# A linear-attention and MLP kernel: the first layer of units 3 to 11 in seven products of 64-row tiles, with its inputs laid out by heads

## The chip, the cores and the metric

The kernel runs on one core of one Trainium2 chip. The metric is the device time of one execution in microseconds (us), the median of several runs. A core has TensorE (PE, matrix products from SBUF into PSUM), VectorE (DVE), ScalarE (ACT), GpSimd (POOL) and SyncE (SP, which here only issues DMAs). Every engine works through its own instructions in order and waits on semaphores for the others.

## What is computed

```python
def _attn_ref(r, k, v, w, u):                    # all (4, 8, 768, 48) float32, u (8, 48)
    for t in range(S):
        cur = np.einsum('bhd,bhe->bhde', u[None] * kt, vt)
        y[:, :, t] = np.einsum('bhd,bhde->bhe', rt, state + cur)
        state = wt[:, :, :, None] * state + np.einsum('bhd,bhe->bhde', kt, vt)
x = y.transpose(0, 2, 1, 3).reshape(3072, 384)
h = x @ w_in                                     # (384, 2048)
out = (h * (1.0 / (1.0 + np.exp(-h)))) @ w_out   # (2048, 384), float32
```

An attention with a decaying state (4 batches, 8 heads of 48, 768 tokens) gives x; two matrix products with a silu between them follow. All is float32.

## The kernel before

**Tiling.** A unit is 128 tokens of two batches, 256 rows of x; six stretches of tokens and two pairs of batches make 12 units, 0 to 11. Attention is not run token by token: decays are multiplied up over 128 tokens, scores (128 x 128 for each head) come from PE, the state enters once a unit. x is kept transposed, features on partitions, 384 = 3 chunks (KC) of 128, 256 columns (two halves of 128, one for each batch).

**Order.** The order is written out by hand and each engine keeps it. Iteration i of the main loop (i from 3) emits in turns the groups of attention steps of unit i (`mix`), and the steps of the second layer of unit i-2 (`downs`: seven `quarter` products) and of the first layer of unit i-1 (`ups`); the tuple `room` says how many matrix steps follow each group. Iterations 0 to 2 are written singly; they also convert the weights (loaded in eight pieces for each matrix, `load_weight`) with `head_weight`, `tail_weight`, `join_weight` and, on GpSimd, `add_weight` (L259).

**Attention steps that matter here.** `turn` transposes r, k and w; `product`, `grow_*`, `prepare` multiply decays (L616 on DVE, L634 and L643 on GpSimd, L604 on ACT); `burst` and `keep_level` make scores (L692, L700 on PE; L710 on DVE; the score copies, L792, on ACT). The bonus u is a chain of its own: `block_bonus` (L491, eight products on GpSimd: four for the next unit ahead of `y_state`, four in this one), `block_sum` (L525, DVE), `block_move` (three DMAs), `block_spread` (L552, four ACT copies and a shuffle on DVE), `block_write` (L561, two predicated DVE copies into the scores). Then `turn_apart` and `turn_k` (kq, the keys for the state, ACT copies from PSUM), `y_state` (L835) and `y_values` (L856) on PE, four ACT copies of y to `yt` (L861), and `update` of the state (L896). `yt` has heads on rows 0 to 47 and 64 to 111; `move_x` (L914) makes x of it with ten DMAs from SBUF to SBUF, for units from 4 on issued by ACT.

**Matrix steps.** Units 0 to 2 run the first layer plainly (`up`, L1011; 24 products of 128 x 128 weights and 256 columns, silu at L1020). From unit 3 on (NFAST) `first_layer` (L1065) splits two of the three chunks with the two batches and the two halves of the 2048 columns after Strassen and Winograd, seven products for eight; the third chunk is folded in plainly. So each half of 1024 columns takes 11 products of 8 tiles, each tile 128 rows x 64 columns of weights by 128 moving columns, two tiles side by side on the two column halves of PE. `sums_of_x` (L1039, DVE, five 128 x 128 subtractions) makes d1 to d4 of x, `in_weight_sums` makes s1, s2, s4 and a21 of w_in once, in iterations 3 and 4. Each product ends in two halves' evacuation: an ACT copy (p1, p6, p5, L1074), a DVE add into gt and an ACT silu (n1, p7, p3, L1077, L1080), or a silu alone (p4, L1082). Four PSUM banks are kept for this: h0, h1 (p_h) and o0, o1 (p_o). The second layer's `sums` (L1127, DVE) and `quarter` (L1156 on PE, evacuations L1161 and below) follow one iteration later.

**Loads.** All loads and stores are issued by SP. Values (`load_values`) have two buffers and are loaded a unit ahead; the blocks of r, k and w are spread over the groups of an iteration.

```python
    for i in range(3, len(units)):
        steps = downs(i - 2) + ups(i - 1)
        groups = mix(i)
        if i - 1 >= NFAST:
            groups[3].append((sums_of_x, i - 1))
...
        for group, count in zip(groups, room):
            do(*group)
            for step in steps[:count]:
                do(*step)
            steps = steps[count:]
```

Of the kernel before, what the change touches and what calls it, by code (L numbers as in the profile page):

```python
# [8 lines left out]
F32 = mybir.dt.float32  # L9
# [29 lines left out]
def kernel(  # L39
# [11 lines left out]
    nc = tc.nc  # L51
# [44 lines left out]
    WRK = {"w": 0, "r": 1, "k": 2}  # L96
    vt, vq, whole = {}, {}, {}
# [32 lines left out]
    def load_values(i):  # L130
# [3 lines left out]
        rooms = [pin.tile([128, H * D + PD - D], F32, name=name, bufs=2) for name in ("vt", "vq")]  # L134
        if n == 0:
            for room in rooms:
                nc.vector.memset(room[:, H * D:], 0.0)
        whole[i] = rooms
        vt[i], vq[i] = (room[:, 0:H * D].rearrange("p (h d) -> p h d", h=H) for room in rooms)
# [66 lines left out]
    def load_weight(i):  # L206
        dst, src = w_ends[i]
        if rounded:
            dst, src = staged(i).rearrange("p (c f) -> p c f", c=src.shape[1]), src.bitcast(U32)
        nc.sync.dma_start(out=dst, in_=src)  # L210
# [603 lines left out]
    def turn_k(i):  # L814
        both_kq = pt.tile([128, NB, NP, 2 * PD], F32, name="kq", bufs=1)
        for b in range(NB):
            kq[i, b] = both_kq[:, b]
        for e, have in enumerate(apart[i]):
            nc.scalar.copy(out=both_kq[:, :, :, PD * e:PD * e + D], in_=have)
# [30 lines left out]
    def y_values(i, e):  # L850
# [7 lines left out]
        if e == 0:  # L858
            yt[i] = pt.tile([128, NP, NB, L], F32, name="yt", bufs=1)
        for x in range(2):  # L860
            nc.scalar.copy(out=yt[i][PD * e:PD * e + D, x::2, :, :],  # L861
                           in_=p_yt[i, e][PD * x:PD * x + D].rearrange("p (q b) t -> p q b t", b=NB))
# [3 lines left out]
    def x_products(i, b):  # L866

        if b == 0:
            xt[i] = pt.tile([128, KC, TU], F32, name="xt", bufs=1)
        to = p_x[i, b] = ps.tile([128, KC, L], F32, name="p_h", bufs=2) if i == 0 else bank("p_m", KC, L)  # L870
        have = whole[i][b]
        places = []
        for c in range(KC):
            for row in range(0, 128, PD):
                at = c * 128 + row
                last = (at + PD - 1) // D
                assert at // D == last - 1
                places += [(c, row, last, PD), (c, row, last - 1, last * D - at)]
        places.sort(key=lambda place: -place[3])
        for c, row, h, columns in places:  # L880
            at = c * 128 + row
            nc.tensor.matmul(to[row:row + columns, c, :], lhsT=have[:, at:at + columns],
                             rhs=score[:, i % NSC, h % 2, b * NP + h // 2, :], start=True, stop=True)
# [4 lines left out]
    def update(i, b):  # L888
# [5 lines left out]
        for p in range(NP):  # L894
            for e in range(2):
                nc.tensor.matmul(p_kv[i][PD * e:PD * e + D, b, p, :], lhsT=kq[i, b][:, p, PD * e:PD * e + D],  # L896
# [17 lines left out]
    def move_x(i, first=0, last=None, queue=nc.sync):  # L914

        if i not in xt:
            xt[i] = pt.tile([128, KC, TU], F32, name="xt", bufs=1)
        moves = []
        for h in range(H):
            at = h * D  # L920
            while at < (h + 1) * D:
                end = min((h + 1) * D, (at // 128 + 1) * 128)
                row = PD * (h % 2) + at - h * D
                moves.append((xt[i][at % 128:at % 128 + end - at, at // 128, :],
                              yt[i][row:row + end - at, h // 2].rearrange("p b t -> p (b t)")))
                at = end
        for to, have in moves[first:last]:
            queue.dma_start(out=to, in_=have)
# [9 lines left out]
    def mix(i):  # L938
# [15 lines left out]
        def start(j):  # L954
# [3 lines left out]
               [*at(i < len(units) - NB, (turn_apart, i), (turn_k, i)), (y_state, i), *both(y_values, i), *at(ahead, *turns(i + 1)),  # L958
                (sums, i - 1, FH // 2 - 2 if i - 1 < NFAST else 0), *both(update, i), *at(not ahead, (move_x, i))]]
# [11 lines left out]
        else:  # L971
            groups = [[*both(turn, i, "r"), (grow_own, i, 0), (move_x, i - 1, 0, 2, nc.scalar)],
                      [*start(i), *sum_steps(i, 0, 1), *bonus_steps(i, 4, 5), (move_x, i - 1, 2, None, nc.scalar)],
# [10 lines left out]
        if i + 1 < len(units):  # L984
            loads.insert(len(loads) // 2, (load_values, i + 1))
# [36 lines left out]
    HALF = DF // 2  # L1022
    whole_w = raw[:, 1].rearrange("p x b h d -> p x (b h d)")
    in_sums = [whole_w[:, WRK["r"]], const.tile([128, HALF], F32, name="in_sum"), whole_w[:, WRK["w"]]]
    a11, a12, a13 = (w_in_sb[:, c, 0:HALF] for c in range(KC))
    a21, a22, a23 = (w_in_sb[:, c, HALF:DF] for c in range(KC))
    x_sums = [spare[:, at + x * L:at + (x + 1) * L] for x in range(3)] + [const.tile([128, L], F32, name="x_sum")]

    def in_weight_sums(which):
        out, one, two, op = ((in_sums[0], a21, a22, ALU.add), (in_sums[1], in_sums[0], a11, ALU.subtract),  # L1030
                             (in_sums[2], a12, in_sums[1], ALU.subtract), (a21, a11, a21, ALU.subtract))[which]
# [284 lines left out]
```

## Time and profile before

| | |
|---|---|
| device time of three runs | 588.21, 590.79, 591.96 us; median 590.79 |
| span of the profiled execution, first to last instruction | 588.6 us (the page gives no other time for it) |
| granted TensorE clock | 1.000 throughout |
| busy in the span | PE 97%, DVE 77%, POOL 60%, ACT 45% |
| 0 to 100 us (units 0, 1, weights converted) | PE 93.98 busy |
| 100 to 189.37 us (to the start of unit 3's first layer) | PE 88.34 of 89.37 busy |
| seven stretches from one unit's first layer to the next, 189.37 to 505.33 | 45.58, 44.34, 45.82, 45.58, 45.31, 44.52, 44.81 us |
| the last such stretch, 505.33 to 547.44 | 42.11 us, all of it PE busy |
| tail, 547.44 to 588.60 | PE 37.83 busy |

The stretches are read from the chain of waits, in which every unit's p1 starts with the same row, and their busy times from a table of windows. An engine's idle time is put down to what released it ("<-PE p_sc L692"). "PEld" is the loading of weights, which runs beside the products. A float32 product is recorded as two passes, so the profile counts 8070 where the program has 4132 products (a few records are missing).

### The profile page before, as it was taken

What the parts mean: (1) busy time and instruction counts of PE and PEld (TensorE: products, weight loads), DVE (VectorE), ACT (ScalarE), POOL (GpSimd) and SP (SyncE); (2) the same over time, 40 slices, a digit from 0 to 9 for tenths busy, and PEclk for the clock granted to TensorE, in tenths of its full rate; (3) what the DMA queues carried; (4) which work ended last, traced back from release to release, by engine and by line L of the source; (5) the groups of instructions that cost most, each with busy time, mean ns of one, the idle gap of its engine ahead of it and who ended that gap; (6) DMA issues with size and microseconds to landing.
All of it is one profiled execution on the core that took longest, in us unless ns stands there. A gap on an engine that the chain in (4) does not pass through costs nothing.

```text
span 588.6 us, 19384 instructions
## 1 busy us (share of the span) xinstructions
PE 573.7 (97%) x8070; PEld 533.3 (91%) x8070; DVE 455.7 (77%) x703; ACT 264.2 (45%) x582; POOL 354.1 (60%) x415
## 2 busy tenths in 40 slices
PE   8989999999999999999999999999999989999997
PEld 8767876798899989999999989999999989999997
DVE  7979789998898898787788898888678797861150
ACT  5679694431531561561561561460470462370320
POOL 5989778357768478287486496485676677500000
PEclk9999999999999999999999999999999999999999
DMA  9957785343432643544543544444354460100000
GB/s 231 311 122 195 167 244 82 47 86 70 102 68 39 133 71 53 131 66 75 114 68 60 123 62 68 105 75 73 85 100 71 95 102 27 38 7 24 28 3 26
DMA packets 203383, 53.70 MB, mean 91 GB/s; under 512 B 186784, under 2 KB 195104, under 8 KB 203296
## 3 DMA queue, kind: packets, MB, share of 16 engines
q1 hardware_dynamic: 197360, 48.73, 41.0%
q10 hardware_dynamic: 5936, 3.74, 2.4%
q8 instruction: 63, 1.03, 0.8%
q14 instruction: 24, 0.20, 0.1%
HBM read 43.21 MB, written 5.24 MB: 82 GB/s over the span
## 4 chain that ended last, share of the span: by engine, by line
PE 76%; SPq 5%; DVE 5%; POOL 4%; DMA 4%; ACT 3%; issue 1%; ACTq 1%; POOLq 0%; DVEq 0%
PE p_o L1156 26%; PE p_h L1065 16%; PE p_o L1065 8%; PE p_h L1011 8%; PE p_h L1156 4%; PE p_m L1095 4%; PE p_m L856 2%; PE p_sc L692 2%; DVE score L561 2%; SPq L127 2%; PE p_m L835 2%; DMA vq<-in_v_dram 2%; ACT score L792 2%; POOL w_in_sb L259 2%; POOL tk L634 1%
## 5 line engine op out<-in xcount | busy, mean ns | idle before, releaser
L634 POOL TENSOR_TENSOR tk<-tk,tw 128x256 f32<-128x256 f32 x128 | 91.3, 734 | 42.8 <-ACT tk L604 27.6
L491 POOL TENSOR_TENSOR ruk<-tokens_rk 128x768 f32<-128x768 f32 (+1 forms) x32 | 53.6, 1687 | 70.9 <-DVE block_sums L525 36.6
L1156 PE MATMUL p_o<-own,temps 128*128 128x192 f32 x528 | 88.8, 327 | 1.3 <-ACT partial L1161 1.3
L1156 PEld LDWEIGHTS p_o<-own,temps 128*128 128x128 f32 x528 | 86.0, 190 | 2.5 <-ACT partial L1161 2.4
L1011 PE MATMUL p_h<-xt,w_in_sb 128*128 128x256 f32 x288 | 66.1, 384 | 1.7 <-POOL w_in_sb L259 1.5
L1065 PE MATMUL p_h<-xt,w_in_sb 128*64 128x128 f32 x1008 | 62.8, 274 | 0.4 <-issue 0.4
L1011 PEld LDWEIGHTS p_h<-xt,w_in_sb 128*128 128x128 f32 x288 | 53.6, 190 | 10.0 <-POOL w_in_sb L259 2.4
L1156 PE MATMUL p_o<-w_out_sb,gt 128*128 128x192 f32 x340 | 59.9, 329 | 0.2 <-DVE temps L1127 0.2
L616 DVE TENSOR_TENSOR tr<-tr,tw 128x512 f32<-128x512 f32 x61 | 57.3, 939 | 2.6 <-PE p_m L692 2.1
L1065 PEld LDWEIGHTS p_h<-xt,w_in_sb 128*64 128x64 f32 x1008 | 55.8, 137 | 2.0 <-issue 0.9
L1156 PEld LDWEIGHTS p_o<-w_out_sb,gt 128*128 128x128 f32 x340 | 55.3, 190 | 2.0 <-issue 1.2
L1161 ACT COPY partial<-p_o 128x192 f32<-128x192 f32 x33 | 10.6, 320 | 95.7 <-PE p_o L1156 46.5
L406 POOL TENSOR_TENSOR tw<-tw 128x256 f32<-128x256 f32 (+6 forms) x83 | 40.0, 482 | 17.7 <-DVE tw L360 13.8
L1065 PE MATMUL p_o<-xt,w_in_sb 128*64 128x128 f32 x720 | 46.9, 273 | 0.0
L604 ACT COPY tk<-tk 128x256 f32<-128x256 f32 x52 | 21.2, 407 | 53.8 <-POOL tk L634 49.2
L1065 PEld LDWEIGHTS p_o<-xt,w_in_sb 128*64 128x64 f32 x720 | 40.8, 137 | 0.0
L1074 ACT COPY gt<-p_h 128x512 f32<-128x512 f32 x45 | 26.2, 582 | 30.4 <-PE p_h L1065 30.4
L1080 ACT ACTIVATE gt<-gt 128x512 f32<-128x512 f32 x36 | 22.7, 631 | 34.1 <-DVE gt L1077 33.9
L710 DVE COPY_PREDICATED score<-mask,p_sc 128x512 f32<-128x512 int8 x42 | 31.3, 800 | 5.8 <-PE p_sc L692 5.5
L1077 DVE TENSOR_TENSOR gt<-p_o,gt 128x512 f32<-128x512 f32 x27 | 18.4, 683 | 19.4 <-PE p_o L1065 19.4
L1077 DVE TENSOR_TENSOR gt<-p_h,gt 128x512 f32<-128x512 f32 x27 | 18.6, 687 | 17.3 <-PE p_h L1065 16.2
L643 POOL TENSOR_TENSOR tk<-tk,tw 128x256 f32<-128x256 f32 x32 | 30.9, 986 | 0.0
(225 smaller groups left out, 1272.0 us busy)
## 6 DMA issues: line engine op xcount, KB each, us to landing
w_out_sb<-in_moe_w_in_dram SPq DMA_DIRECT2D x6, 768.0 KB, 7.1
w_out_sb<-in_moe_w_out_dram SPq DMA_DIRECT2D x4, 768.0 KB, 5.1
own<-in_moe_w_out_dram SPq DMA_DIRECT2D x4, 768.0 KB, 5.8
tokens_rk<-in_r_dram SPq DMA_DIRECT2D x8, 384.0 KB, 4.4
tokens_rk<-in_k_dram SPq DMA_DIRECT2D x8, 384.0 KB, 5.3
tokens_w<-in_w_dram SPq DMA_DIRECT2D x8, 384.0 KB, 6.4
raw<-in_w_dram SPq DMA_DIRECT2D x80, 32.0 KB, 2.3
raw<-in_k_dram SPq DMA_DIRECT2D x80, 32.0 KB, 2.1
```

The lines of the kernel that those rows point to most:

```text
L406: engine.tensor_tensor(out=up, in0=t[:, :, 0::2], in1=t[:, :, 1::2], op=ALU.mult)
L491: mul = lambda out, one, two: nc.gpsimd.tensor_tensor(out=out, in0=one, in1=two, op=ALU.mult)
L616: nc.vector.tensor_tensor(out=odd, in0=odd, in1=tw[i][l][:, :, 0::2][:, :, :, None].to_broadcast([128, Q, L >> (l + 1), c]), op=ALU.mult)
L634: nc.gpsimd.tensor_tensor(out=out, in0=have, in1=odd_products(i, l, b, *blocks), op=ALU.mult)
L643: nc.gpsimd.tensor_tensor(out=have, in0=have, in1=odd_products(i, l, b, [2, NP * ni]), op=ALU.mult)
L710: nc.vector.copy_predicated(out=dst, mask=masks[l][:, :, None].to_broadcast([128, NB, NP, ni, c]), data=sc[e].rearrange("p (b q) (i c) -> ...
L1011: nc.tensor.matmul(p_h[:, a, :], lhsT=w_in_sb[:, c, f * 128:(f + 1) * 128], rhs=xt[i][:, c, :], start=(c == 0), stop=(c == KC - 1))
L1065: nc.tensor.matmul(p[h:h + PD, q, :], lhsT=left[:, f:f + PD], rhs=right, start=first and n == 0 and q == 0, stop=last and n == len(pairs) ...
L1074: nc.scalar.copy(out=g(*{"p1": (0, 0), "p6": (0, 1), "p5": (1, 1)}[name]), in_=p)
L1077: nc.vector.tensor_tensor(out=to, in0=p, in1=to, op=ALU.add)
L1095: nc.tensor.matmul(po[i, b], lhsT=gt[i, f // 2][:, f % 2, b * L:(b + 1) * L], rhs=w_out_sb[:, f, :], start=(f == 0), stop=(f == FC - 1))
L1156: nc.tensor.matmul(p, lhsT=left(f), rhs=right[:, f, :], start=which in (0, 1, 3) and f == 0, stop=f == FH - 1, skip_group_check=True)
```

## The change

From unit 3 on all three chunks are split. x and the rows of w_in are laid out by heads: chunk c has head 2c on rows 0 to 47 and head 2c+1 on rows 64 to 111, and 16-row slices of heads 6 and 7 on rows 48 to 63 and 112 to 127. `load_weight` reads w_in in four DMAs for a piece in place of one, in that order of rows. The 64-row halves of this layout are the inner split of the products: `first_layer` has seven products (p1, p2, p6, p5, p7, p3, p4), each of 3 chunks x 4 blocks of 128 columns x 2 halves of the outer columns, in tiles of 64 rows x 128 columns; the two halves alternate between the two row halves of PE and go to two PSUM banks. For that, the two 64-row halves of some blocks of w_in change places once (`swap_out` in iteration 3, `swap_in` in iteration 4: DMAs within SBUF), and each half of x is copied to the other row half as well (`spread_x`, two ACT copies a unit). `in_weight_sums` is now two DVE operations of 128 x 1536 and, on GpSimd, one of 128 x 1536 and three of 128 x 512, all in iteration 4. `sums_of_x` is four subtractions of 128 x 384 and stands in group 4, behind the block sums and `block_move`, where it stood in group 3.

y goes from PSUM straight into x (`x_rooms`) for six of eight heads, by ACT (`y_out`, six copies); only heads 6 and 7 pass through `yt`, and `move_x` is six DMAs of 16 rows on SP. For units 0 and 1 `x_products` writes the new layout. Values have one buffer and are loaded within their own unit's iteration; the other loads are spread anew over the groups. s3 of the second layer is kept in gt's place in SBUF, so the quarter sums take three parts of `temps` in place of four. The eighth entry of `room` is 1 where it was 2, since a unit has seven first-layer steps in place of eight.

```diff
@@ load_weight (columns of w_in, i < NW)
+        columns = moe_w_in[:, i * 256:(i + 1) * 256]
+        upper = columns[0:2 * KC * D, :].rearrange("(c e p) f -> e p c f", c=KC, e=2)
+        lower = columns[2 * KC * D:, :].rearrange("(e c p) f -> e p c f", c=KC, e=2)
+        for e in range(2):
+            for first, last, have in ((PD * e, PD * e + D, upper[e]), (PD * e + D, PD * e + PD, lower[e])):
+                nc.sync.dma_start(out=dst[first:last], in_=have.bitcast(U32) if rounded else have)
...
@@ load_values
-        rooms = [pin.tile([128, H * D + PD - D], F32, name=name, bufs=2) for name in ("vt", "vq")]
+        have = (s1_room if i == 1 else value_rooms).rearrange("p x d -> p (x d)")
+        rooms = [have[:, b * H * D:(b + 1) * H * D] for b in range(NB)]
...
@@ y_values, y_out
-        if e == 0:
-            yt[i] = pt.tile([128, NP, NB, L], F32, name="yt", bufs=1)
-        for x in range(2):
-            nc.scalar.copy(out=yt[i][PD * e:PD * e + D, x::2, :, :],
-                           in_=p_yt[i, e][PD * x:PD * x + D].rearrange("p (q b) t -> p q b t", b=NB))
+    def y_out(i):
+        xt[i] = x_rooms[:, 0]
+        yt[i] = pt.tile([128, TU], F32, name="yt", bufs=1)
+        for e in range(2):
+            rows, to = slice(PD * e, PD * e + D), x_rooms[PD * e:PD * e + D, e if i >= NFAST else 0]
+            have = [p_yt[i, e][PD * x:PD * x + D].rearrange("p (q b) t -> p q (b t)", b=NB) for x in range(2)]
+            nc.scalar.copy(out=to[:, 0::2], in_=have[0])
+            nc.scalar.copy(out=yt[i][rows], in_=have[1][:, 1])
+            nc.scalar.copy(out=to[:, 1], in_=have[1][:, 0])
...
@@ move_x, spread_x
-        moves = []
-        for h in range(H):
...
-        for to, have in moves[first:last]:
-            queue.dma_start(out=to, in_=have)
+        for e in range(2):
+            rows = slice(PD * e + D, PD * e + PD)
+            for c in range(KC):
+                first = PD * e + 16 * c
+                queue.dma_start(out=x_rooms[rows, e if i >= NFAST else 0, c], in_=yt[i][first:first + 16])
+
+    def spread_x(i):
+        for x, rows in enumerate((slice(0, PD), slice(PD, 2 * PD))):
+            to = slice(PD - PD * x, 2 * PD - PD * x)
+            nc.scalar.copy(out=x_rooms[to, x], in_=x_rooms[rows, x])
...
@@ mix, groups of units from 4 on
-            groups = [[*both(turn, i, "r"), (grow_own, i, 0), (move_x, i - 1, 0, 2, nc.scalar)],
-                      [*start(i), *sum_steps(i, 0, 1), *bonus_steps(i, 4, 5), (move_x, i - 1, 2, None, nc.scalar)],
+            groups = [[*both(turn, i, "r"), (grow_own, i, 0), (move_x, i - 1)],
+                      [*start(i), *sum_steps(i, 0, 1), *bonus_steps(i, 4, 5)],
...
+            for place, some in enumerate(("w", "ww", "wvr", "r", "", "rr", "k", "k", "k", "k")):
...
@@ swap_out, swap_in, in_weight_sums, sums_of_x
+    def swap_out(x, queue=nc.sync):
+        for rows, other, block in ((slice(0, PD), slice(PD, 128), 2 * x), (slice(PD, 128), slice(0, PD), 2 * x + 1)):
+            queue.dma_start(out=swap_rooms[x][rows], in_=blocks_w[block][other])
+
+    def swap_in(x, queue=nc.sync):
+        for rows, block in ((slice(0, PD), 2 * x + 1), (slice(PD, 128), 2 * x)):
+            queue.dma_start(out=blocks_w[block][rows], in_=swap_rooms[x][rows])
...
-        (b11, b12), (b21, b22), (b31, b32) = (tuple(xt[i][:, c, b * L:(b + 1) * L] for b in range(NB)) for c in range(KC))
-        d1, d2, d4, d3 = x_sums
-        for out, one, two in ((d1, b12, b11), (d2, b22, d1), (b12, b22, b12), (d4, b21, d2), (d3, b31, b32)):
+        b11, b12, b21, b22 = parts_of_x()
+        for out, one, two in ((d1, b12, b11), (d2, b22, d1), (b12, b22, b12), (d4, b21, d2)):
             nc.vector.tensor_tensor(out=out, in0=one, in1=two, op=ALU.subtract)
...
@@ first_layer
-            place, first, last, pairs = {
-                "p1": ("x", True, True, [(a11, b11)]), "p6": ("x", False, True, [(s2, d2)]), "p7": ("x", False, True, [(a21, b12), (a23, b32)]),
-                "p4": ("x", False, True, [(a22, d4), (a23, d3)]), "p5": ("y", True, True, [(s1, d1)]),
-                "p3": ("y", False, True, [(s4, b22), (a13, b32)]), "p2": ("z", True, False, [(a12, b21)]),
-                "n1": ("z", False, True, [(a13, b31)])}[name]
...
+        place, first, last, left, right = {
+            "p1": ("h", True, True, a11, b11), "p6": ("h", False, True, s2, d2), "p7": ("h", False, True, a21, b12),
+            "p4": ("h", False, True, a22, d4), "p2": ("o", True, True, a12, b21), "p5": ("o", True, True, s1, d1),
+            "p3": ("o", False, True, None, b22)}[name]
+        banks_of = [kept[f"{place}{half}"][:].rearrange("p (q t) -> p q t", q=4) for half in range(2)]
+        for c in range(KC):
+            weights = s4[c][:, 0] if left is None else left[:, c]
+            for q in range(4):
+                for half in range(2):
+                    rows = slice(PD * half, PD * half + PD)
+                    nc.tensor.matmul(banks_of[half][:, q, :], lhsT=weights[rows, q * 128:(q + 1) * 128],
+                                     rhs=right[rows, c], start=first and c == 0 and q == 0,
+                                     stop=last and c == KC - 1 and q == 3, skip_group_check=True)
...
@@ ups
-            order = (((0, "p1"), (0, "p5"), (0, "p2")), ((0, "p6"), (0, "n1"), (1, "p1")), ((0, "p7"), (0, "p3")),
-                     ((0, "p4"), (1, "p2"), (1, "p6")), ((1, "p5"), (1, "n1")), ((1, "p7"),), ((1, "p3"),), ((1, "p4"),))
+            made = [[(first_layer, i, name)] for name in ("p1", "p2", "p6", "p5", "p7", "p3", "p4")]
...
@@ main loop
-            groups[3].append((sums_of_x, i - 1))
+            groups[3].append((spread_x, i - 1))
+            groups[4].append((sums_of_x, i - 1))
...
+            groups[5].append((swap_out, 1))
+            groups[6].append((swap_out, 0))
...
+            groups[0] += [(swap_in, 0), (swap_in, 1)]
+            groups[2].append((in_weight_sums, 0))
+            groups[3].insert(0, (in_weight_sums, 1))
+            groups[5].append((in_weight_sums, 3))
+            groups[6].append((in_weight_sums, 2))
-        room = (1, 1, 0, 2, 1, 1, 1, 1, 1, 2, 2, 1, 1) if i < NPAIR else (2, 1, 2, 2, 1, 1, 1, 2, 1, 1, 1)
+        room = (1, 1, 0, 2, 1, 1, 1, 1, 1, 2, 2, 1, 1) if i < NPAIR else (2, 1, 2, 2, 1, 1, 1, 1, 1, 1, 1)
```

## The prediction

> **What bounds the kernel now.** I read the page's busy shares first, then the chain of waits in order of time, then the timeline of one unit per engine. TensorE is busy 97% of the span, and the chain stands on it for 76%.
>
> ```profile
> PE 573.7 (97%) x8070; PEld 533.3 (91%) x8070; DVE 455.7 (77%) x703; ACT 264.2 (45%) x582; POOL 354.1 (60%) x415
> ...
> PE 76%; SPq 5%; DVE 5%; POOL 4%; DMA 4%; ACT 3%; issue 1%; ACTq 1%; POOLq 0%; DVEq 0%
> ```
>
> The chain (start, length, what) shows the rhythm: each unit's first layer starts with the same row, at 189.37, 234.95, 279.29, 325.11, 370.69, 416.00, 460.52 and 505.33.
>
> ```profile
> 189.37 1.02 PE p_h L1065 x16
> ...
> 193.89 2.62 PE p_h L1065 x48
> ...
> 325.11 1.02 PE p_h L1065 x16
> ...
> 336.90 4.15 DVE score L561 x2
> 345.92 1.09 PE p_m L835 x28
> ...
> 505.33 1.02 PE p_h L1065 x16
> ```
>
> Seven units take 505.33 - 189.37 = 315.96 us, 45.14 each. The reader should see two things: long unbroken PE rows, and in the unit of 325 a detour over VectorE (block_write, L561) that ends in y_state (L835). VectorE's chain is thus almost as late as PE's in three of these units (201, 337 and 472 have the 4.15 row).
>
> **The first layer's products.** A unit issues 11 products of 8 tiles for each half, 176 tiles, and would issue 7 x 3 x 4 x 2 = 168. The records show two passes for a tile, and tiles of the two halves run side by side, so a tile costs half a pair of each pass: 48 records in 2.62 us are 24 pairs of 109.2 ns. A product of 64-row, 128-column tiles is not in the trace, but the level products of L700 have the same form: 48 rows, 128 columns, 128 moving, two row halves and two banks in turn. These two timeline rows are its weight loads and those of the present form:
>
> ```profile
> 104.28 0.97 PEld L700 LDWEIGHTS p_o<-tr,tk 48*128 48x128 f32 x16
> ```
>
> ```profile
> 235.69 0.91 PEld L1065 LDWEIGHTS p_o<-spare,raw 128*64 128x64 f32 x16
> ```
>
> One L700 load lasts 0.188, so 7 intervals fill 0.97 - 0.188: 111.7 ns a pair. That is the value I take; the other end is 109.2. A unit goes from 176 x 109.2 = 19.22 to 168 x 111.7 = 18.77 us: 0.45 less, 4.1 us over nine units (at 109.2: 18.35, 7.9 less). One product becomes 24 pairs, 2.68 us.
>
> The Trainium skill ("TensorE: Matmul & The Clock Gate", LDWEIGHTS) says that a load takes its columns over 1.2 GHz whatever the rows: 106.7 ns for 128, under the 109.2 of a pair, so by it loads would stay hidden and the gain would be the 7.9. The L700 row contradicts that by 2.5 ns a pair. A rule that speaks against the change is in "TensorEngine Tiling (Array Packing)", PSUM Pressure: row tiles need different PSUM banks. The change does hold two banks for each product; no run here shows yet what this costs.
>
> **What the other engines do inside one unit.** I follow the after order from T, the start of product p1, with the rows of the unit that starts at 279.22:
>
> ```profile
> 278.88 1.33 DVE L710 COPY_PREDICATED score<-mask,p_sc 128x512 f32<-128x512 int8 x2 [1.70 <-PE p_sc L692]
> 280.11 0.93 DVE L525 TENSOR_REDUCE block_sums<-spare 128x16 f32<-128x768 f32 x1
> 280.95 0.95 DVE L525 TENSOR_REDUCE block_sums<-ruk 128x16 f32<-128x768 f32 x1
> 281.81 1.35 DVE L710 COPY_PREDICATED score<-mask,p_m 128x512 f32<-128x512 int8 x2
> 283.05 0.96 DVE L616 TENSOR_TENSOR tr<-tr,tw 128x512 f32<-128x512 f32 x1
> 283.93 0.69 DVE L1077 TENSOR_TENSOR gt<-p_o,gt 128x512 f32<-128x512 f32 x1
> ```
>
> The first add of a product now starts at T+4.71. In the changed order sums_of_x, which stood ahead of this block, stands in its middle: four subtractions of 384 columns. Their price: 128x1536 took 1.75 (L1113), 128x1024 1.21 (L1032), so 1.05 ns a column and 0.53 for 384. The other end is 1.91, from a 128x128 one that ended with a GpSimd instruction running beside it:
>
> ```profile
> 322.33 1.91 DVE L1039 TENSOR_TENSOR spare<-xt,spare 128x128 f32<-128x128 f32 x1
> ```
>
> I take 0.53, as GpSimd then waits for ScalarE's copy of odd keys: 2.1 together. p2's two adds end at T+4.71+2.1+1.30 = T+8.1. p5 overwrites the banks that they read, and PE is there at 3 x 2.68 = T+8.04: a wait of 0.1 to 0.2 (at 1.91 each, 5.6).
>
> ScalarE is next and runs in order: two silus to 8.85, odd keys and tr copy to 9.7, two p6 copies to 10.7, the spread copies and shuffle (289.55 to 291.09 now) to 12.2. Then block_write takes 2.5, to T+14.7, or 4.1 where GpSimd's bonus products (L491) start between its two instructions, to T+16.3. The 12 score copies (294.74 to 298.41) end at T+18.5 or T+20.1, and only then are the banks of y_state free. PE arrives at 6 x 2.68 + 1.09 (burst) + 0.62 (transposes) + 0.15 = T+17.9, where it came at T+20.3 before: the last product behind y_state grew from 1.75 to 2.68, and there is less in front. **The new wait** is 0.6 or 2.2 us. Behind it stand four silus (2.2) and two kq copies (0.86) on ScalarE where two silus stood, 3.15 with the latency; y_state and y_values last 2.64 (299.56 to 302.20). The update waits 0.5 and starts at T+21.7 or T+23.3. After it: update 0.72, p4 2.68, seven quarters 18.5, burst 1.09, together 23.0. A unit takes 44.7 or 46.3, against 45.14. With four of one kind and three of the other, as L561 shows them now, seven units change by 4 x -0.44 + 3 x 1.16 = +1.7 us.
>
> **What goes.** ScalarE no longer issues the ten xt moves of a unit. Now it stalls on them:
>
> ```profile
> ACT partial L1161 <- DMA xt<-yt: 45.4, 9, 7.6
> ```
>
> PE pays little of that: 1.3 us in waits for L1161 (0.50 ahead of 315.95), inside the 45.14 already. Six moves on SP instead stand ahead of the next loads; an issue takes 0.45 to 0.6, and SP idles at the unit's end. If SP were full they would delay x by some 3 us, against 20 us of quarters.
>
> **Moved or added, hidden.** y_out writes x in six ScalarE copies in place of four (2.4 now, some 2.9): it lies behind kq, and x is read a unit later. It needs p3's reads of the old x, which PE has issued before y_state. spread_x (two copies of 64x768, 0.9 each from 0.62 for 512 columns) falls into ScalarE's idle time of 3.3 to 4.5 ahead of the last quarter. The value tiles are single: the load waits for the last update, lands in about 4 us (vt 4.2) and is needed two dozen us later; uncovered it would cost 4 a unit. Removed memsets, the other order of unit 2's up-products and s3 in gt leave work and critical order as they are.
>
> **Once only.** In the first unit of the new kind GpSimd gets a 128x1536 subtraction (two of 1.85 for 768, so 3.7) just when sums_of_x starts. By the 1.91 row above VectorE waits for it: 3.6 more by p5. The swaps of the weight halves (four DMAs out, four in) lie under 13 us of quarters. Bounds 0 to 5; I take 3.0. At the start w_in comes in 32 DMAs instead of 8; SP issues take 0.45, so 24 more are 10.8 us of SP, but it waits now for landings by about as much (single issues of 2.2 to 5.6 us before 32). A block lands 2.6 to 9 us ahead of its use; only the token load of unit 2 is waited for (GpSimd, 2.8). Bounds 0 to 4; I take 0.5. The last unit and the tail have neither bonus products nor loads: -0.45 and -0.05.
>
> **Sum.** 1.7 + 3.0 + 0.5 - 0.5 = +4.7 on the span of 588.6, so 593.3. The median of the runs, 590.79, is 2.2 above that span; against it I forecast 595.5, with a chance of 0.38 for this case. About 1% is what a measurement of this kernel tells from no change.
>
> **Rivals.**
> - PE stays the bound (0.22). For it: 97% busy, and ScalarE is only 45% busy. Then the waits at y_state and kq do not appear; 4.1 to 7.9 go from products and up to 5 from the present stalls (45.14 against 44.3 in the unit of 234.95, the one without). With 0 to 3 back for the start: 578 to 585, 581 likeliest.
> - ScalarE's and VectorE's chain takes over in every unit (0.38), the other sign: all seven units meet GpSimd's bonus products within block_write, as the new order lets the token loads start earlier (block sums end at T+2.6; 4.2 where x sums were late). 7 x 1.16 = 8.1, plus 3.6 and 1 to 4: 603. It decides from the point where block_write ends later than T+14.2. If the x sums cost 1.04 each, as a 128x512 sum of L1127 does, another 2 a unit: 618. Against it: GpSimd's start at T+12.8 to 13.7 is a close race.
> - The tiles do not run side by side (0.02): 5 us a product, over 700 us. The L700 row speaks against it.
>
> **Numbers.** The range goes from 581, the first rival's middle, to 608, inside the second; about 2 in 10 lie outside. Faster by over 1% is the first rival, 0.22; within 1% the forecast, 0.38; slower by over 1% the second and third, 0.40.
>
> **What would show it.** Right: L700's rate in the products (2.68 each), a y_state that waits for the score copies, units of 44.7 and 46.3, a first unit longer by 3. Wrong: units below 44.2, which puts PE at the bound; a wait ahead of p5 above 1 us, which means that the x sums met GpSimd; or PE waits before 100 us that are not there now, which means the split loads.

## The result and the profile after

The changed kernel takes 612.85 us (median of 604.58, 612.74, 612.96 and 614.21) against 591.38 for the kernel before: 612.85 / 591.38 is 1.036. The ratio of the fast runs alone, which leaves out the 614.21 as a slow one, is 1.0332, 95% interval 1.0255 to 1.041. The forecast was 595.5 with a range of 581 to 608. Its profiled execution has a span of 611.2 us, 22.6 more than the 588.6 before.

Four lines of the page, which answer to the busy line and the chain of before: the busy shares, TensorE's and VectorE's slices, and the granted clock in tenths.

```profile
PE 590.5 (97%) x7926; PEld 542.7 (89%) x7926; DVE 436.9 (71%) x688; ACT 277.6 (45%) x620; POOL 361.9 (59%) x419
...
PE   8798999999999879999999999999999999999997
...
DVE  7738939899777688579589489589589579572250
...
PEclk9898999999999879999999999999999999999999
```

TensorE is again 97% busy, so this share says nothing on what went wrong. But the clock is below full in slices 2, 4, 14 and 15, and there TensorE is idle too: the places to look at are the start and the stretch around 200 to 230 us. The starts of p1 in the timeline of each kernel give the same answer in numbers (from the first record of a unit's first layer to that of the next). Unit 3's p1 after, where before has it at 189.30:

```profile
210.56 2.95 PE L1103 MATMUL p_h<-x_rooms,w_in_sb 64*128 64x128 f32 x48
```

| stretch | before | after | difference |
|---|---|---|---|
| start to unit 3's first layer | 189.30 | 210.56 | +21.3 |
| unit 3 | 45.58 | 50.88 | +5.3 |
| units 4 to 10, sum | 312.49 | 309.06 | -3.4 |
| from unit 11's first layer to the end | 41.2 | 40.7 | -0.5 |

So the steady units got faster, and everything lost lies in what happens once.

**The steady units.** The timeline of a unit after, TensorE alone (start, length, line, operation):

```profile
350.44 2.95 PE L1103 MATMUL p_h<-x_rooms,w_in_sb 64*128 64x128 f32 x48
353.22 2.85 PE L1103 MATMUL p_o<-x_rooms,w_in_sb 64*128 64x128 f32 x48
355.90 2.85 PE L1103 MATMUL p_h<-spare,raw 64*128 64x128 f32 x48
358.58 2.85 PE L1103 MATMUL p_o<-spare,in_sum 64*128 64x128 f32 x48
...
371.96 1.30 PE L906 MATMUL p_sc<-values,kq 128*48 128x48 f32 x32 [0.24 <-ACT kq L829]
```

A product follows the one before it by 2.68 (2.78 behind p1), which is 24 pairs of 111.7 ns: the price taken from L700. p5 (358.58) does not wait. The one visible wait is that of the update for the kq copies. Units 4 to 9 last 43.87, 45.13, 45.12, 45.12, 45.12, 43.11 (unit 9 has fewer attention steps behind it, unit 10 fewer still: 41.59). Two kinds, as forecast; what tells them apart is block_write. First the 43.87 unit, then a 45.12 one, VectorE and GpSimd:

```profile
273.07 2.51 DVE L571 COPY_PREDICATED score<-spare 128x1024 f32<-128x1024 int8 x2
275.24 1.98 POOL L501 TENSOR_TENSOR ruk<-tokens_rk 128x768 f32<-128x768 f32 x1 [3.78 <-DMA tokens_rk<-in_k_dram]
...
362.07 4.11 DVE L571 COPY_PREDICATED score<-spare 128x1024 f32<-128x1024 int8 x2
362.36 2.65 POOL L501 TENSOR_TENSOR ruk<-tokens_rk 128x768 f32<-128x768 f32 x1 [1.90 <-DMA tokens_rk<-in_k_dram]
```

Where the tokens land 0.3 to 0.9 us behind the start of block_write (units 5 to 8), GpSimd runs beside it and block_write takes 1.6 us longer. The score copies on ScalarE wait for it, first for its first instruction and then for its second:

```profile
363.47 1.06 ACT L802 COPY score<-p_sc 32x128 f32<-32x128 f32 x4 [0.74 <-DVE score L571]
366.27 1.06 ACT L802 COPY score<-p_sc 32x128 f32<-32x128 f32 x4 [1.74 <-DVE score L571]
```

**The start.** The products of x of unit 0, before and after, and two of the weight loads after:

```profile
28.09 1.66 PE L882 MATMUL p_h<-score,vt 128*64 128x128 f32 x24
29.68 1.66 PE L882 MATMUL p_h<-score,vq 128*64 128x128 f32 x24
```

```profile
32.65 8.29 PE L892 MATMUL p_h<-score,values 128*32 128x128 f32 x48
...
32.98 0.16 PEld L892 LDWEIGHTS p_h<-score,values 128*48 128x48 f32 x2 [0.20 <-issue]
33.33 0.14 PEld L892 LDWEIGHTS p_h<-score,values 128*32 128x32 f32 x2 [0.18 <-issue]
```

The same 48 records take 8.29 us where they took 3.25, and 8.28 for 3.24 in unit 1: 10.1 us. Before them 4.6 us more are lost, most of which these rows show, TensorE's again:

```profile
22.21 1.16 PE L710 MATMUL p_sc<-tr,tk 48*128 48x128 f32 x16
...
26.45 0.91 PE L408 MATMUL p_m<-values,partial 128*128 128x384 f32 x2 [2.05 <-DMA values<-in_v_dram]
27.29 2.08 PE L710 MATMUL p_h<-tr,tk 48*128 48x128 f32 x16
```

A wait for the values of unit 0, and behind it the same 16 records take 2.08 in place of 1.16; the granted clock from 25 to 30 us is 0.73. The last quarters of unit 1 then stall, from 186.81 to 210.56, 23.75 where before took 19.39 (169.91 to 189.30). VectorE and then TensorE:

```profile
202.41 2.47 DVE L1065 TENSOR_TENSOR in_sum<-w_in_sb 128x1536 f32<-128x1536 f32 x1 [4.64 <-DMA w_in_sb<-in_sum]
204.80 0.34 DVE L1213 TENSOR_TENSOR ob<-p_o,partial 128x192 f32<-128x192 f32 x1
```

```profile
205.20 4.34 PE L1205 MATMUL p_o<-w_out_sb,gt 128*128 128x192 f32 x16 [2.63 <-DVE ob L1213]
```

VectorE stands at its first sum of w_in for the swapped halves. The evacuation of a quarter is behind it in VectorE's order, and the next quarter needs the bank.

**The first new unit.** In unit 3 the first sum of x meets GpSimd's sum of w_in, and product p5 waits and then runs slowly. VectorE, GpSimd and TensorE:

```profile
213.14 2.30 DVE L1077 TENSOR_TENSOR spare<-x_rooms 128x384 f32<-128x384 f32 x1
```

```profile
211.57 3.45 POOL L1065 TENSOR_TENSOR w_in_sb<-w_in_sb 128x1536 f32<-128x1536 f32 x1
```

```profile
222.32 6.09 PE L1103 MATMUL p_o<-spare,in_sum 64*128 64x128 f32 x48 [2.90 <-DVE gt L1121]
```

The granted clock from 220 to 230 us is 0.63 to 0.69.

### The profile page after: what moved, and what is told of

The parts are those of the page before. It is cut to its first block, busy times and chain, and to the rows that moved or that the text cites. A ratio compares the mean times of both kernels' runs of the same rounds, so it can differ in the third digit from the quotient of the medians.

```text
span 611.2 us, 19253 instructions
## 1 busy us (share of the span) xinstructions
PE 590.5 (97%) x7926; PEld 542.7 (89%) x7926; DVE 436.9 (71%) x688; ACT 277.6 (45%) x620; POOL 361.9 (59%) x419
## 5 line engine op out<-in xcount | busy, mean ns | idle before, releaser
L501 POOL TENSOR_TENSOR ruk<-tokens_rk 128x768 f32<-128x768 f32 (+1 forms) x32 | 52.9, 1662 | 43.0 <-DVE block_sums L535 22.5
L1030 PE MATMUL p_h<-x_rooms,w_in_sb 128*128 128x256 f32 x288 | 67.3, 389 | 0.5 <-ACT gt L1039 0.2
L1030 PEld LDWEIGHTS p_h<-x_rooms,w_in_sb 128*128 128x128 f32 x288 | 54.3, 193 | 9.2 <-ACT gt L1039 0.8
L1205 PE MATMUL p_o<-own,temps 128*128 128x192 f32 x352 | 59.0, 326 | 0.0
L1205 PEld LDWEIGHTS p_o<-own,temps 128*128 128x128 f32 x352 | 57.5, 190 | 0.0
L1103 PE MATMUL p_h<-x_rooms,w_in_sb 64*128 64x128 f32 x864 | 53.1, 276 | 0.0
L1103 PEld LDWEIGHTS p_h<-x_rooms,w_in_sb 64*128 64x128 f32 x864 | 49.7, 188 | 1.3 <-issue 0.2
L1116 ACT COPY gt<-p_h 128x512 f32<-128x512 f32 x36 | 19.2, 585 | 32.4 <-PE p_h L1103 32.4
L1103 PE MATMUL p_o<-spare,in_sum 64*128 64x128 f32 x432 | 28.9, 289 | 2.9 <-DVE gt L1121 2.9
L1103 PEld LDWEIGHTS p_o<-spare,in_sum 64*128 64x128 f32 x432 | 27.8, 204 | 3.2 <-DVE gt L1121 3.1
L1205 PE MATMUL p_o<-w_out_sb,temps 128*128 128x192 f32 x176 | 30.4, 326 | 0.0
```

What stands on the lines that cost most here:

```text
L501: mul = lambda out, one, two: nc.gpsimd.tensor_tensor(out=out, in0=one, in1=two, op=ALU.mult)
L1030: nc.tensor.matmul(p_h[:, a, :], lhsT=w_in_sb[:, c, f * 128:(f + 1) * 128], rhs=xt[i][:, c, :], start=(c == 0), stop=(c == KC - 1))
L1103: nc.tensor.matmul(banks_of[half][:, q, :], lhsT=weights[rows, q * 128:(q + 1) * 128], rhs=right[rows, c], start=first and c == 0 and q == ...
L1205: nc.tensor.matmul(p, lhsT=left(f), rhs=right[:, f, :], start=which in (0, 1, 3) and f == 0, stop=f == FH - 1, skip_group_check=True)
```

## The experiments

Ratios are against the kernel before, run on the same chip. "Start" is the start of unit 3's first layer in the trace, one execution each. It scatters by some 3.5 us: the runs e20, e22 and e25 below have the same steps up to there and start at 192.74, 189.26 and 190.52.

### The products of x: how wide, and in which order

```diff
- for c, e:  32 columns at row 32, then 48 at row 0   (12 products, widths in turns)
+ e1_sorted: the six of 32 first, then the six of 48, in turns on the two column halves
+ e1_wide:   the old order, 64 columns at row 0 in place of 32 at row 32
```

> The changed kernel, with the products of x of units 0 and 1 reordered: first the six of 32 columns, then the six of 48, in turns on the two column halves. In the changed kernel they alternate 32 and 48, and 48 records took 8.29 and 8.2 us where the kernel before took 3.24. Theory A (going from a tile of up to 32 columns to one of up to 64 and back costs some 0.2 us each time: 24 changes in 5.0 us) and theory B (two products in a row on the same column half do not run side by side) both expect 3.2 to 3.6 us for each unit and 9 to 10 us off the whole. If the new layout of x or of the values were the cause, it would stay at 8.2.

> The changed kernel in its own order, but each product of 32 columns made one of 64 columns (its first 48 rows are overwritten by the next product, as in the kernel before). Theory A (change of tile width): 3.3 to 5.2 us for 48 records, since every product is now of the same width class. Theory B (same column half twice in a row): 8 us as in the changed kernel.

Both make the products as fast as before; one row of each timeline:

```profile
32.40 3.21 PE L893 MATMUL p_h<-score,values 128*32 128x128 f32 x48
```

```profile
30.16 2.87 PE L892 MATMUL p_h<-score,values 128*64 128x128 f32 x48
```

In the wide run two products in a row still go to the same column half, so theory B falls. The edit changes the starting row together with the width (row 0 for row 32). The kernel before tells the two apart: there every product starts at row 0 or 64, and its weight loads stop at each change of width:

```profile
29.12 0.35 PEld L882 LDWEIGHTS p_h<-score,vt 128*32 128x32 f32 x8 [0.18 <-issue]
29.68 0.84 PEld L882 LDWEIGHTS p_h<-score,vq 128*64 128x64 f32 x16 [0.21 <-issue]
```

So it is the change of width. With 23 changes among 24 products it costs (8.29 - 2.87) / 23 = 0.24 us each, the 0.18 to 0.20 us of idle ahead of each load included. The Trainium skill ("TensorEngine Tiling (Array Packing)", Key Properties) says that a change of the tiling mode drains TensorE; the idle time at each change fits that, and these runs give the price.

But the whole gained little. With the wide products: 611.32 in one run, start 206.84 (changed kernel 210.56). With the sorted ones: 614.39, ratio 1.0386 (1.0332 to 1.0439), start 213.75, no better than the changed kernel. Some 5 us less in each of two places, and at most 3.7 of the 10 arrive. Two rows of the wide run say where it stayed, ACT's conversion of a piece of w_in and GpSimd's bonus of unit 2:

```profile
56.87 0.91 ACT L237 ACTIVATE temps<-w_out_sb 128x768 bf16<-128x768 bf16 x1 [4.82 <-DMA w_out_sb<-in_moe_w_in_dram]
```

```profile
80.12 1.00 POOL L442 TENSOR_TENSOR spare<-tokens_rk 128x384 f32<-128x384 f32 x1 [11.24 <-DMA tokens_rk<-in_k_dram]
```

In the kernel before, the first wait is not there, and the second is short:

```profile
64.81 1.00 POOL L432 TENSOR_TENSOR spare<-tokens_rk 128x384 f32<-128x384 f32 x1 [1.61 <-DMA tokens_rk<-in_k_dram]
```

In the changed kernel these waits are 0.56 and 11.16. The loads were late all along, under the slow products.

### The loads of w_in

```diff
- nc.sync.dma_start(out=dst, in_=src)                          # before: 128 rows
+ e10_before_split:  four DMAs, rows 0-47, 48-63, 64-111, 112-127
+ e11_before_chunks: three DMAs, chunk 0, 1, 2, 128 rows each
+ e18_before_halves: two DMAs, rows 0-63, 64-127
```

All three are the kernel before with this one edit, the old order of rows kept.

> The kernel before, and only the loads of w_in cut as the changed kernel cuts them: four DMAs of 48, 16, 48 and 16 rows for a piece, in the old order of rows. Theory C (loads that cover only part of the rows move fewer bytes per us, so everything behind them on SP lands late): 5 us windows in which the DMA engines are full show some 215 GB/s in place of 330, the blocks and tokens of unit 2 land 10 us later, and 6 to 11 us are lost before unit 3's first layer. The prediction's step (issues hidden under landings): 0.5, at most 2.

> The kernel before, and only the loads of w_in cut into three DMAs for a piece, one for each chunk, each over all 128 rows: 16 more issues, where the changed kernel has 24 more. Theory C (it is the rows covered): as the kernel before, 0 to 2 us more, and 300 GB/s and more in full windows. Rival D (it is the number of issues on SP and of DMAs outstanding): two thirds of what the cut into rows costs, 4 to 7 us.

> The kernel before, and only the loads of w_in cut into two DMAs for a piece, rows 0 to 63 and rows 64 to 127: 8 more issues, half as many as the cut into chunks, which cost nothing. If it is the rows that a DMA covers, full windows show some 215 GB/s as in the cut into 48 and 16 rows, and 6 to 14 us are lost before unit 3's first layer (13.6 there). If it is the number of DMAs, nothing is lost. The Trainium skill (SBUF - State Buffer, The DMA port swizzle) says that 64 rows reach half of the ports, which speaks for the first.

| | DMAs a piece | us, median | ratio (95%) | start | GB/s at 25 to 30 us |
|---|---|---|---|---|---|
| before | 1 | | | 189.30 | 333 |
| chunks | 3 | 591.13 | 0.9964 (0.9921 to 1.0007) | 189.23 | 314 |
| halves | 2 | 603.01 | 1.0135 (1.0073 to 1.0197) | 200.86 | 213 |
| 48 and 16 rows | 4 | 605.63 | 1.0160 (1.0075 to 1.0246) | 202.94 | 183 |

The last column is from the table of windows; before, chunks, halves and the cut into 48 and 16 rows in turn (the last two columns are the share of the DMA engines and GB/s):

```profile
25.00:30.00 5.00, 4.86 (x100) 3.94 (x98) 3.90 (x6) 3.40 (x9) 5.00 (x7) 1.00 1.07 333
```

```profile
25.00:30.00 5.00, 4.86 (x100) 4.04 (x100) 3.90 (x6) 3.60 (x9) 5.00 (x6) 1.00 0.96 314
```

```profile
25.00:30.00 5.00, 4.99 (x103) 4.10 (x100) 3.90 (x6) 3.89 (x10) 5.00 (x6) 1.00 0.98 213
```

```profile
25.00:30.00 5.00, 4.86 (x95) 3.97 (x94) 3.12 (x5) 4.75 (x12) 4.19 (x5) 1.00 1.01 183
```

The DMA engines are full in all four, and with part of the rows they move 0.55 to 0.64 as much. Sixteen more issues over all rows cost nothing, eight more over half of the rows cost 11.6 us of start. Rival D falls: it is the rows that a DMA covers. The cut into 48 and 16 rows costs 13.6 us in its trace, more than the 6 to 11 expected; the ratio of its runs puts it at 9.5 us (4.4 to 14.6), that of the halves at 8.0 (4.3 to 11.7). With this the loads are the largest single cost in the traces, and the products of x hid a part of it: 13.6, 10.1 for the products and 4.4 for the stall add up to 28.1, of which 21.3 appear together. The Trainium skill ("SBUF — State Buffer", The DMA port swizzle) says that 64 rows of one half reach 8 of 16 ports; the 213 against 333 agree in direction, at 0.64 of the rate and not half.

Loading the values one place earlier, in the changed kernel, was the small end of the same matter:

> The changed kernel with the loads of the values of unit 0 issued ahead of the second piece of w_in. Theory: four DMAs for a piece put these loads from 12.77 to 17.44 us, TensorE waits 2.05 us for them at 24.4 and then runs at a lower granted clock; here the loads are issued at about 14.4, the wait goes and with it 2 to 4.5 us of the 4.6 that unit 0 lost before its products of x. Rival: the converted pieces of w_in become the wait instead, and less than 1 us is won.

The products of x then begin at 30.77 in place of 32.65, and the time is 612.14 (ratio 1.0302, 1.0216 to 1.0389), which cannot be told from the changed kernel: the rival was right. TensorE now waits 1.71 for a copy on ScalarE, which itself had stood 2.64 for a piece of w_in.

### The swap and the first new unit

```diff
- iteration 4, group 0:  behind move_x: (swap_in, 0), (swap_in, 1)
+ iteration 3, group 11: (swap_in, 1);  behind the last product of unit 2: (swap_in, 0)
```

> The changed kernel with the weight halves swapped in earlier: the one of the upper columns in iteration 3, as soon as unit 2 has read them, the other one right after unit 2's last product, ahead of the moves of x. Theory: VectorE stands 4.64 us at its first sum of w_in for the swap, the second layer's evacuation waits behind it, TensorE idles 2.63 us and then runs at a lower clock; all that goes: 4.4 us ahead of unit 3's first layer, and some of the 7.0 us by which unit 3 is longer than the next unit (part of that is the lower clock): 5 to 8 in all. Rival: the sums meet GpSimd wherever they are, and only 2 to 3 us are won.

607.86 us, ratio 1.0263 (1.0205 to 1.0321). The quarters take 19.38 again (188.01 to 207.39), so the 4.4 are shown to be the swap; the start itself comes 3.2 earlier. Unit 3 stays at 50.66, which is the other half of the rival. GpSimd's sum of w_in, VectorE's second sum of x, and the two products that wait:

```profile
210.91 3.76 POOL L1065 TENSOR_TENSOR w_in_sb<-w_in_sb 128x1536 f32<-128x1536 f32 x1
```

```profile
211.48 3.61 DVE L1077 TENSOR_TENSOR spare<-x_rooms,spare 128x384 f32<-128x384 f32 x1
```

```profile
215.24 4.58 PE L1103 MATMUL p_h<-spare,raw 64*128 64x128 f32 x48 [2.22 <-DVE spare L1077]
220.44 3.54 PE L1103 MATMUL p_o<-spare,in_sum 64*128 64x128 f32 x48 [0.64 <-DVE gt L1121]
```

The sum of x ends 0.4 behind GpSimd's, 3.61 in place of 0.55. Besides the wait of 2.22 the two products take 4.58 and 3.54 in place of 2.95 and 2.85: after an idle time of 2.2 us TensorE ran slowly for a while (granted clock 0.66 from 215 to 220 us).

### All of it together

```diff
+ e5_fixed:    wide products, values earlier, early swap, GpSimd's sum of w_in behind the sums of x
+ e12_natural: the same without the earlier values, w_in in one DMA a piece, old order of rows
+             (the permutation is left out: the rows of w_in do not match those of x)
```

> The changed kernel in full, with the products of x all 64 columns wide, the loads of unit 0's values one place earlier, the weight halves swapped in early, GpSimd's sum of w_in behind the sums of x; w_in still in four DMAs a piece. Theory: 4 us of the products of x (the loads hide the rest, as in the run with the wide products), 4.4 of the evacuation and 5 of unit 3 come off: a span of 595 to 599.

> The changed kernel with four things taken back or moved: w_in loaded in one DMA for a piece in the old order of rows (so the rows of w_in no longer match those of x: the permutation is left out), products of x all 64 columns wide, the weight halves swapped in early, GpSimd's sum of w_in behind the sums of x. Theory: the four cover the whole loss. Unit 3's first layer starts at 189 to 192 (210.6 in the changed kernel), its unit lasts 44 to 46 (50.9), the rest as in the changed kernel (349.8 to the end): a span of 583 to 588, 3 us or so under the kernel before. If something else of the change also costs, it stays above 592.

With the four DMAs kept: 609.08, ratio 1.0209 (1.0133 to 1.0285), a span of 607.2 and so 8 to 12 us above what was expected: the start is 203.83 (210.6 less the 4 and 4.4 would be 202.2), unit 3 takes 49.1, and units 4 and 8 are 2 us longer each. With one DMA: 593.13, ratio 0.9981 (0.9939 to 1.0022), start 188.17, unit 3 in 46.39. Between these two traces lie 15.7 us of start, which is the price of the cut loads once more, here by taking them away; the earlier values, in the first alone, could only make it smaller. The 21.3 us are accounted for, though their shares overlap. The span of 593.9 was above the expected 588 because of unit 4, 50.52 in that trace. SP had a backlog there: the moves of the bonus sums, whose sums ended at 237, were issued at 245.31 to 248, and TensorE waited 3.94 us behind them.

### The products without the layout

w_in and x in the natural order of features need no cut loads. The inner split is then rows 0 to 63 and 64 to 127 of the natural order.

```diff
+ e20_products: load_weight and x_products as before; y_out: even heads PSUM -> x (six ACT copies),
+               odd heads -> yt (two), move_x: six DMAs; early swap, late GpSimd sum
+ e21, e22:     load_rk behind one more load_blocks of group 5   (e21 leaves out the tokens of unit 5)
+ e25:          e22, and in iteration 5 the two blocks of r (eight loads) that stood ahead of block_move behind it
+ e23, e24:     the late load_rk alone, in the kernel before and in the changed one
```

> The seven products of 64-row tiles without the layout by heads: w_in in one DMA a piece and x in the natural order of features, as in the kernel before. Products of x as before. From unit 2 on the even heads of y are copied from PSUM into x (six copies), the odd ones go through yt and six DMAs on SP. Early swap, GpSimd's sum of w_in late, as in the run with natural loads. Theory: the whole loss lay in the layout and in the one-time work; unit 3's first layer starts at 188 to 190, its unit lasts 44 to 47, the next ones 43.9 to 45.2, the last 41.6: a span of 582 to 590, 0 to 1% under the kernel before. Rival: something of the steady units costs too, and it ends above 592.

> As the run before it, and the loads of the next unit's tokens stand behind one more block of loads on SP, so that GpSimd's first bonus product begins some 2 us later, after block_write. Theory: the units of 45.1, in which block_write takes 4.1, become units of 43.9 with 2.5: 3 to 5 us under the run before it. Rival: GpSimd's later products meet other VectorE work, and the sum is the same within 1 us.

> The run with the natural order and late token loads again, with the token load of unit 5 put back, which that run had left out (so its bonus was computed from old tokens). Theory: the units stay at 43.9, unit 4 may cost up to 1.2 more: 584 to 587, 0.9 to 1.3% under the kernel before.

> The kernel before, and only the token loads of units 6 to 11 put behind one more block of loads on SP. Its trace shows the long block_write in three units of eight, 1.2 us each. Theory: 2 to 4 us off, 588 to 590. Rival: nothing, as its product ahead of y_state ends later than the score copies anyway.

> The changed kernel, and only the token loads put behind one more block of loads on SP. Theory: the four units of 45.1 become units of 43.9: 4 to 5 us under the changed kernel, some 608; the loss before 260 us stays.

> The repaired run with natural order and late token loads, and in iteration 5 alone twelve of SP's loads of r (three blocks) stand behind the moves of the bonus sums instead of ahead of them. There its unit 4 took 49.9 us, as the moves were issued at 247 to 251 (block sums ready some 8 us earlier) and TensorE waited 3.6 us behind them. Theory: unit 4 becomes one of 43.9 to 45.2, 4 to 6 us off: 582 to 585, 1.2 to 1.7% under the kernel before. Rival: the late loads of r hold up the next unit by as much.

| | us, median | ratio (95%) | unit 3 | unit 4 | units 5 to 8 |
|---|---|---|---|---|---|
| e20_products | 593.44 | 1.0010 (0.9984 to 1.0036) | 49.31 | 44.45 | 43.87, 45.14, 43.87, 46.27 |
| e21_products_late | 585.16 | 0.9882 (0.9849 to 0.9916) | 46.40 | 44.50 | 45.32, then 43.87 |
| e22_products_late2 | 588.40 | 0.9937 (0.9912 to 0.9962) | 46.39 | 49.85 | 43.87 four times |
| e25_products_first | 586.68 | 0.9893 (0.9860 to 0.9927) | 49.32 | 43.88 | 44.90, 45.43, 43.87, 43.87 |
| e23_before_late | 587.19 | 0.9941 (0.9911 to 0.9970) | 45.57 | 44.93 | 44.56, 44.19, 44.66, 45.69 |
| e24_after_late | 608.31 | 1.0245 (1.0184 to 1.0306) | 49.81 | 44.03 | 45.64, then 43.87 |

e20 missed its 582 to 590: its start of 192.74, unit 3 and unit 8 are all longer than expected. e21 is 8.3 us faster, but only 2.2 of this lie in units 5 to 8; most of the rest is the start and unit 3, and it leaves out a load of tokens. e22 and e25 end 1.4 and 1.7 us above what was expected. The edit of e25 moves eight loads of r, two blocks, where the text ahead of the run says twelve.

The late token loads settle what the two kinds of unit are. In the changed kernel with this one edit, VectorE and GpSimd:

```profile
363.05 2.50 DVE L571 COPY_PREDICATED score<-spare 128x1024 f32<-128x1024 int8 x2
```

```profile
367.56 1.83 POOL L501 TENSOR_TENSOR ruk<-tokens_rk 128x768 f32<-128x768 f32 x1 [6.13 <-DMA tokens_rk<-in_k_dram]
```

GpSimd waits 6.13 instead of 1.90, block_write is free, and three of the four units of 45.1 become units of 43.87. Units 5 to 8 together take 177.26 in place of 180.49, 3.2 us less; 4 to 5 were expected of the whole, and the medians differ by 4.5, though the intervals of the two ratios overlap. In e22 the one long unit was SP's order, ACT waiting for the moved bonus sums:

```profile
251.58 0.24 ACT L562 COPY spare<-spare 128x64 f32<-128x64 f32 x1 [5.76 <-DMA spare<-kept]
```

In e25 that unit is 43.88, but unit 3 varies between 46.4 and 49.3 from trace to trace with the same steps in it. Product p5 of unit 3, first in e22 and then in e25:

```profile
198.17 3.54 PE L1119 MATMUL p_o<-spare,in_sum 64*128 64x128 f32 x48 [0.60 <-DVE gt L1137]
```

```profile
201.00 4.91 PE L1121 MATMUL p_o<-spare,in_sum 64*128 64x128 f32 x48 [2.18 <-DVE gt L1139]
```

The long ones (e20 and e25) wait 2.18 there: their block sums wait 1.0 and 0.8 for GpSimd's bonus products (L501), where those of e22 wait 0.6 in all, and the sums of x stand behind them. What makes GpSimd late in one execution and not in another was not pursued. e25 beats both kernels: 1.1% under the kernel before. About half of this is the order of the loads, which by itself gives the kernel before 0.6%; the two were run on different chips, so their difference is only rough.

## Why the prediction was wrong

The sum said +4.7 us on the span, and +22.6 were measured. Its terms for the start and the first new unit were far too small; its term for the steady units was too large.

- **A step that was left out.** The prediction had no term for the products of x of units 0 and 1. The section on the change names them, in one sentence on the layout. Rows of 32 and 48 columns in turn cost 10.1 us.
- **"w_in comes in 32 DMAs instead of 8 ... Bounds 0 to 4; I take 0.5."** This counted issues, and the run with chunks shows that issues are indeed free. The rows covered by a DMA were not considered: by itself 13.6 us in the trace, 9.5 by the runs. Of the cover that was named ("a block lands 2.6 to 9 us ahead of its use") nothing was left, as tokens and later pieces stand behind these loads on SP: GpSimd waits 11.16 for the tokens of unit 2.
- **"The swaps of the weight halves ... lie under 13 us of quarters."** They did in time, but VectorE's sums wait for them in VectorE's order, ahead of two evacuations of these same quarters: 4.4 us. What is queued behind a waiting instruction was asked for PE and ACT, not here.
- **The first new unit, "3.6 more by p5" (with the swaps "I take 3.0").** The overlap that it named is there: beside GpSimd's work the four sums of x take 5.6 us in all in place of 2.1, and in the run with the early swap one of them takes 3.61 for 0.55. The size was not right: 50.88 is 7.0 above the next unit. TensorE ran below full clock behind its wait, and the delay is also in VectorE's later steps. Nor is GpSimd's sum the whole cause: with it moved behind the sums of x, unit 3 takes 46.4 in three traces and 49.1 to 49.3 in three others, where the block sums wait longer for GpSimd's bonus products. That part stays open.
- **The steady units, "44.7 or 46.3", +1.7 in all.** Measured 43.87 and 45.12; units 4 to 10 took 3.4 us less, 0.5 of it in unit 10, where -0.45 was said. The products were right: 2.68 each, the price from L700 (109.2 a pair would be 2.62), and the two banks of each product cost nothing that can be seen. From the Trainium skill ("TensorE: Matmul & The Clock Gate", LDWEIGHTS) comes an estimate of 106.7 ns for a load of 128 columns; pairs came here every 111.7. Right were also the sums of x (0.55 for 0.53) and the two kinds of unit. The mis-sized term is the wait at y_state: block_write began at T+11.6 (T+12.2 was worked out), and the score copies were put behind both of its instructions, where the first four start after the first one. They end at T+16.8 and T+18.4 in place of T+18.5 and T+20.1; TensorE arrives at T+18.0, where T+17.9 was said. So a free unit has no wait, and a contended one takes 1.25 us more, over y_state, y_values and the update.
- **The rivals.** The measured 612.85 lies within the 603 to 618 of the second rival, but not by its mechanism: it had all seven units meet GpSimd within block_write, and four did. In the free units it was the first rival that held, with TensorE as the bound; units 4 to 10 and the tail gave 3.9 us, where it had 4.1 to 7.9 from the products alone.

## What to carry to other kernels

A change of layout is paid where the data is made and loaded, once or not: write down a price for every line that the diff touches, the ones outside the hot loop first, and ask of each DMA which rows it fills. When two things run late side by side, taking one away shows little; put each alone into the old kernel to learn its price. And when a cost falls on an engine that has slack, look for what stands behind it in that engine's order.

## What the runs showed of the chip

- With the loads of w_in going to 64 of 128 rows at a time, 213 GB/s were moved from 25 to 30 us, where loads into all rows moved 333 (314 in three DMAs), with the DMA engines equally full; with 48 and 16 rows in turn, 183.
- Going between tiles of 32 and of 64 columns on TensorE costs about 0.24 us each time when every product does it (8.29 against 2.87 us, 23 changes).
- After 2.0 to 2.2 us of idle TensorE ran slower for a while: 16 records in 2.08 us for 1.16 (granted clock 0.73 from 25 to 30 us), a product in 4.58 for 2.95 (0.66 from 215 to 220).
- A predicated copy of 128x1024 on VectorE took 4.11 us for its two instructions with a GpSimd product running beside it and 2.50 without.
